# Batch 0's keys turned two tokens at a time and earlier; batch 1's values loaded ahead of W2's last quarter

## The chip, the cores and the metric

The kernel runs on one core of one Trainium2 chip. The metric is device time in microseconds, from launch to end. The engines are named as the profile names them: PE (TensorE, products), PEld (its weight loads), DVE (VectorE), ACT (ScalarE), POOL (GpSimd) and SP (SyncE, which only issues transfers here).

## The reference

Two layers follow each other. The first is attention in blocks, in which keys and values are mixed between blocks by a matrix P (five rounds of exp and of row and column scaling of `sort_net`):

```python
k_sorted = np.einsum('bhij,bhjcd->bhicd', P, k_b)      # v_sorted likewise
scores = scale * np.matmul(q_b, k_sb.transpose(0, 1, 2, 4, 3))
attn = np.exp(scores) / sum(np.exp(scores))            # in each block of 96 tokens
x = np.matmul(attn, v_sb)
```

The second is a residual MLP with affine scalings:

```python
a1 = alpha1 * x + beta1
u = x + lam * (w_tok @ a1)                             # over the 768 tokens
a2 = alpha2 * u + beta2
out = u + lam * (np.maximum(a2 @ w_ch1, 0.0) @ w_ch2)  # 512 -> 2048 -> 512
```

There are 4 batches, 8 heads, 768 tokens in 8 blocks of 96, and 64 channels a head. Inputs and output are float32.

## The kernel before, in words

**Order.** The Python program writes one stream of instructions for each engine, and a wrapper (`Engine`, L55) holds each engine to the order in which the calls stand. Its line, L65, is the one that nearly all rows of the profile carry, so rows are told apart by their tiles. Waits between engines are put in by the framework from who writes and who reads which tile. Which buffer of a pool a tile gets is also decided there.

**Accumulators.** Products go to two pools of accumulators: `psA` with 2 large ones (two banks each) and `psB` with 4 small ones (one bank each). `psa(...)` and `psb(...)` take one. A new tile waits until the readers of the tile that had its buffer are done.

**Batch 0's attention** is unlike that of the other batches, as it starts with nothing loaded. Heads go in pairs, four groups g = 0 to 3. For each group:
- `k_turn` (L387, `turn_slab` L238): keys times the mixing matrix `bigK`, which transposes them on the way. A token's keys of one head (64 rows by 64 channels) are the weights, one product a token and head: 24 products of 64x64 weights a group, into two small accumulators.
- `k_copy` (L390): two copies of 128x384 (one on DVE, one on ACT) put the turned keys into `KT0`, laid out by token.
- `score` (L414): 8 products for each half hf of the blocks, then the exp on ACT, in one instruction of 768 columns if the product went to a large accumulator, in two of 384 if it went to two small ones.
- `pv_first` (L464): attention times values, 24 products into a large accumulator, then on DVE a reciprocal and a scaling that write `x128`.

In source the turn of groups 0 and 1 stands ahead of the scores of groups 0 and 1 (L923 to L942). Then come `prep_scales` (two small DVE operations, read from the first `tok_copy` on), POOL's loads, `pv_first(0)`, and only then the turn and the copies of groups 2 and 3 (L960 to L965) and their scores. The scores of group 1 go to small accumulators, with one product on zeros (a filler, L421) ahead of them.

After that come `wtok` (transposes of `w_tok`, copied by DVE and ACT), `first_mm` (the first token products) and the rest of the MLP, which is planned by hand: `put(b, hf, "h" or "c", n, f)` hangs a piece of other work behind the n-th step of the hidden (`h`) or output (`c`) products. The next batch's attention is spread over these steps.

**Loads.** POOL issues nearly all of them, in source order: q, v and k of batch 0, `w_tok`, three scale vectors, W1 in four quarters, W2 in four quarters (L956), then for batch 1 the values, the keys (`load_kv(1)`, L987) and the queries. The values of batch 1 are first used by `mix_v(1, 0)` behind step h 13 of batch 0; the W2 quarters by `scale_weights(g)` on DVE at steps h 10, 11, 12 and 12 (L1061).

Of the kernel before, what the change touches and what calls it, by code (L numbers as in the profile page):

```python
# [7 lines left out]
FT = mybir.dt.float32  # L8
# [8 lines left out]
def kernel(  # L17
# [31 lines left out]
    HB = BLK // 2  # L49
# [23 lines left out]
    pe = Engine(nc.tensor)  # L73
    dve = Engine(nc.vector)
    act = Engine(nc.scalar)
# [11 lines left out]
    def psa(shape, dtype, name):  # L87
        return pools["psA"].tile(shape, dtype, name=name, tag="psA")

    def psb(shape, dtype, name):  # L90
        return pools["psB"].tile(shape, dtype, name=name, tag="psB")

    def const(shape, dtype, name):
        return wts.tile(shape, dtype, name=name, tag=name)

    wz = const([128, 512], F16, "wz")
# [13 lines left out]
    KT0 = att.tile([128, H4, NB, 128], F16, name="kT0", tag="tw", bufs=2)  # L110
# [3 lines left out]
    k8 = att.tile([128, H4, 12 * D], F16, name="k8", tag="raw", bufs=2)  # L114
# [77 lines left out]
                qn_of[b][:, kt, :, :], q[b, :, kt * 128:(kt + 1) * 128, :].rearrange("h p d -> p h d"),  # L192
            )

    def load_kv(b):
        for kv, src in ((1, v), (0, k)):
            raw = att.tile([128, HB, D], F16, name="raw", tag="raw", bufs=2)
            load_halves(raw, src[b])
            raw_of[(b, kv)] = raw
# [72 lines left out]
    def prep_scales():  # L272
        dve.tensor_tensor(
            ab2col[:, 3 * CT:4 * CT], ab2col[:, 2 * CT:3 * CT], ab2col[:, 3 * CT:4 * CT], ALU.mult
        )
        dve.tensor_tensor(ab2col[:, 4 * CT:5 * CT], ab2col[:, 0:CT], ab2col[:, 3 * CT:4 * CT], ALU.mult)
# [44 lines left out]
    bigK = {}  # L321
# [65 lines left out]
    def k_turn(b, g, ps):  # L387
        return turn_slab(k8, lambda r, g: bigK[b][r, g, :], g, "k_ps", ps)

    def k_copy(b, g, ps, half, eng):  # L390
        eng(
            KT0[:, g, :, :].rearrange("p i (th u) -> p (i th) u", th=2)[:, :, 0:HB].rearrange(
                "p x (c t) -> p x c t", t=12
            )[:, :, :, half * 6:half * 6 + 6],
            ps[half].rearrange("p (t x c) -> p x c t", t=6, c=4),
        )

    def v_mm(b, n, out_):
        for s in range(8):
            for th in range(2):  # L400
                d = (s + 4 * th) % 8
                r = slice(th * 64, th * 64 + 64)
                pe.matmul(
                    out_[r, d * 64:d * 64 + 64], VD[r, n * 8 + d, :],
                    bigV[b][r, :, :].rearrange("p h i -> p (h i)"), start=True, stop=True,
                )
# [54 lines left out]
        dve.tensor_tensor(dst, x_of[b][rows, kts, c], al, ALU.mult)  # L461
        dve.tensor_tensor(dst, dst, be, ALU.add)

    def pv_first(g):  # L464
        if g == 0:
            x_of[0] = moep.tile([128, 8, C], F16, name="x128", tag="x128", bufs=1)
        ps = psa([128, 2, 512], FT, "x_ps")[:, :, 0:480].rearrange("p a (k d) -> p a k d", d=80)
        for i in range(NB):
            for h2 in range(2):
                et = ets[(0, g, i // 4)][:].rearrange("p a i t -> p (a i t)")  # L470
                lo = (4 * h2 + i % 4) * BLK
                w = min(128, 8 * BLK - lo)
                val = Vs[:, (2 * g + h2) * NB + i, 0:D + 1]
                if i < 6:
                    pe.matmul(ps[0:w, h2, i, 0:D + 1], et[:, lo:lo + w], val, start=True, stop=True)
                else:
                    for a in range(3):
                        pe.matmul(
                            ps[96:128, h2, 3 * (i - 6) + a, 0:D + 1], et[:, lo + a * 32:lo + (a + 1) * 32], val,
                            start=True, stop=True,  # L480
                        )
        rc = att.tile([128, 2, 6], FT, name="rc", tag="rc", bufs=3)
        dve.reciprocal(rc[:], ps[:, :, :, D])
        dve.tensor_tensor(
            x_of[0][:, 0:NT, g * 128:(g + 1) * 128].rearrange("p k (a d) -> p k a d", a=2),
            ps[:, :, :, 0:D].rearrange("p a k d -> p k a d"),
            rc[:].rearrange("p a k -> p k a").unsqueeze(3).to_broadcast([128, NT, 2, D]), ALU.mult,
        )
# [406 lines left out]
    copy = dve.tensor_copy  # L895
# [42 lines left out]
    k_copy(0, 1, kp1, 1, act.copy)  # L938
    score(0, 0, 0, psa)
    score(0, 0, 1, psa)  # L940
    score(0, 1, 0, psb, 1)
    score(0, 1, 1, psb)  # L942
    prep_scales()
    pool.tensor_tensor(brow[0:1, :], bet1[:], lam1[:], ALU.mult)
    for j in range(1, 4):
        sp.dma_start(brow[32 * j:32 * j + 1, :], brow[0:1, :])
# [7 lines left out]
        pool.dma_start(W1p[:, :, g * 512:(g + 1) * 512], w1v[:, :, g * 512:(g + 1) * 512])  # L954
    permute(1, pool.tensor_copy, 0, 6)
    for g in range(4):  # L956
        pool.dma_start(W2p[:, g * 4:(g + 1) * 4, :], w2v[:, g * 4:(g + 1) * 4, :])
    moe_start(0)
    a1_of[0] = moep.tile([128, 8, C], F16, name="a1", tag="a1", bufs=1)
    pv_first(0)  # L960
    kp2 = k_turn(0, 2, psb)
    kp3 = k_turn(0, 3, psb)
    for g, kp in ((2, kp2), (3, kp3)):
        k_copy(0, g, kp, 0, copy)
        k_copy(0, g, kp, 1, act.copy)  # L965
    score(0, 2, 0, psa)
    score(0, 2, 1, psb)
    pv_first(1)
# [15 lines left out]
    first_turn(2, psa)  # L984
    scale_affine(betaB)

    load_kv(1)  # L987
    load_q(1)
    pool.memset(Vs[0:BLK, :, D:GRP], 1.0)

# [23 lines left out]
    for b in range(1, B):  # L1014
        p = b - 1
# [42 lines left out]
        put(b, 0, "h", 4, lambda b=b: moe_cross(b, 1))  # L1058
        put(b, 0, "c", 2, lambda b=b: moe_affine(b, 1))

    for g, m in enumerate((10, 11, 12, 12)):  # L1061
        put(0, 0, "h", m, lambda g=g: scale_weights(g))
    for n, at_ in enumerate(((0, 1, "c", 4),) * 3 + ((0, 1, "c", 5),) * 3 + ((0, 1, "c", 6),) * 2):
        put(*at_, lambda n=n: block_weights(n))
# [68 lines left out]
```

## Time and profile before

| what | us |
|---|---|
| timed runs: median (lowest to highest) of 3 | 258.17 (256.55 to 260.22) |
| the profiled execution | 256.33 |
| its span, first to last instruction | 254.6 |
| PE busy in the span | 244.0 (96%) |
| DVE, ACT, POOL busy | 174.1 (68%), 155.7 (61%), 46.1 (18%) |
| mean granted PE clock | 0.993 of full |

The profile is one execution. Its page has numbered parts: 1 is busy time, 2 cuts the span into 40 equal slices (a digit is the busy share in tenths, PEclk the granted clock in tenths), 4 is the chain of work that ended last, 5 the costliest groups. In the rows of the timeline the two numbers in front are start and duration, `xN` is the number of instructions merged into the row, and the brackets name the idle time before it and who ended it; "issue" there means that the engine waited for nothing that the profile shows.

The stretch around the change, from the timeline of before (us from the start of the span):

| work | start | length |
|---|---|---|
| scores of group 0 | 16.77 | 0.59 |
| filler, scores of group 1 | 17.29, 18.13 | 0.91, 0.51 |
| six exps of groups 0 and 1 | 17.25 | 3.05 |
| attention product of group 0 | 18.58 | 1.02 |
| turn of groups 2 and 3: one product, then 47 | 19.53, 21.22 | 0.21, 0.94 |
| their four copies, on ACT and DVE | 21.79 | 1.06 |
| scores of group 2 | 22.54 | 0.63 |
| attention product of group 1 | 23.09 | 1.64 |
| scores of group 3, transposes of `w_tok` | 24.66, 25.42 | 0.82, 1.59 |
| first token product | 26.95 | 1.14 |

### The profile page before, as it was taken

To read this page: it belongs to the slowest core of one execution; us is meant where nothing else is said; L and a number is where in the kernel's file an instruction comes from. 1 tells how busy PE (TensorE), PEld (TensorE's weight loads), DVE (VectorE), ACT (ScalarE), POOL (GpSimd) and SP (SyncE) were. 2 spreads that over 40 slices of the span, in tenths; PEclk is the share of its full clock that TensorE was granted. 3 is DMA by queue.
4 is the path that set the end of the run, shared out by engine and by line. 5 is a ranking of instruction groups with operands and counts; after the bars stand their busy time and mean duration, and the time that the engine had idled before them with its cause. 6 is when DMAs were issued, how large, how long until landed. Compare 5 with 4: busy or idle time off the path is not lost.

```text
span 254.6 us, 6059 instructions
## 1 busy us (share of the span) xinstructions
PE 244.0 (96%) x2416; PEld 159.7 (63%) x2416; DVE 174.1 (68%) x461; ACT 155.7 (61%) x285; POOL 46.1 (18%) x70
## 2 busy tenths in 40 slices
PE   7897999999999999999999999999999999999994
PEld 2475765555465545556765797558756875686783
DVE  5884588667379868279896685398978862462773
ACT  4796675567788679786564696878364005837400
POOL 8699604000082010191000010000000000000000
PEclk9997999999999999999999999999999999999999
DMA  5999999998999997999961179710203132111023
GB/s 98 202 210 192 207 205 210 216 179 197 165 179 180 131 209 124 178 159 164 136 161 39 31 189 127 141 23 0 85 0 66 50 115 45 21 41 44 0 85 82
DMA packets 61936, 31.09 MB, mean 122 GB/s; under 512 B 50562, under 2 KB 57618, under 8 KB 61908
## 3 DMA queue, kind: packets, MB, share of 16 engines
q0 software_dynamic: 20976, 16.91, 45.7%
q1 hardware_dynamic: 40836, 13.76, 32.0%
q8 instruction: 19, 0.31, 0.5%
q14 instruction: 9, 0.07, 0.1%
q10 hardware_dynamic: 96, 0.03, 0.1%
HBM read 32.79 MB, written 8.65 MB: 163 GB/s over the span
## 4 chain that ended last, share of the span: by engine, by line
PE 77%; DVE 9%; ACT 6%; DMA 3%; issue 2%; POOL 1%; DVEq 0%; ACTq 0%; POOLq 0%
PE h_ps L65 28%; PE tok_ps L65 12%; PE px L65 8%; PE ch_ps L65 8%; PE pz L65 6%; PE py L65 5%; DMA v<-in_v_dram 3%; PE x_ps L65 3%; DVE x L65 3%; PE sc_ps L65 2%; DVE sums L65 2%; PE kmix_ps L65 2%; PE mix_ps L65 2%; ACT kT L65 1%; ACT vd L65 1%
## 5 line engine op out<-in xcount | busy, mean ns | idle before, releaser
L65 PE MATMUL h_ps<-a2T,W1p 128*128 128x384 bf16 x512 | 93.4, 326 | 0.3 <-DVE a2T L65 0.3
L65 PEld LDWEIGHTS <-W1p 128*128 128x128 bf16 x512 | 47.8, 98 | 30.7
L65 ACT ACTIVATE hTa<-h_ps 128x384 f16<-128x384 f32 x64 | 31.2, 490 | 30.6 <-PE h_ps L65 29.5
L65 ACT ACTIVATE hTb<-h_ps 128x384 f16<-128x384 f32 x64 | 31.3, 489 | 8.7 <-PE h_ps L65 8.7
L65 DVE SCALAR_TENSOR_TENSOR u<-tok_ps,x 128x512 f32<-128x512 f32 x21 | 14.5, 692 | 27.0 <-PE tok_ps L65 27.0
L65 PE MATMUL tok_ps<-a,w_tokT 128*128 128x512 f16 x126 | 30.3, 379 | 0.0
L65 ACT CAST kT<-kmix_ps 64x512 f16<-64x512 f32 x36 | 25.7, 713 | 7.0 <-PE kmix_ps L65 6.5
L65 ACT ACTIVATE et<-sc_ps 96x768 f16<-96x768 f32 (+2 forms) x36 | 24.6, 736 | 2.4 <-PE sc_ps L65 2.4
L65 ACT CAST u<-u 128x512 f16<-128x512 f32 x21 | 13.0, 618 | 20.4 <-DVE u L65 20.4
L65 PEld LDWEIGHTS <-sums 128*128 128x128 f16 x216 | 21.1, 98 | 3.8 <-issue 0.7
L65 PEld LDWEIGHTS <-hTa 128*128 128x128 f16 x192 | 18.2, 98 | 6.6
L65 PEld LDWEIGHTS <-hTb 128*128 128x128 f16 x200 | 18.5, 98 | 6.1
L65 PEld LDWEIGHTS <-w_tokT 128*128 128x128 f16 x126 | 12.3, 98 | 13.1 <-DVE a L65 0.3
L65 DVE TENSOR_TENSOR x<-x_ps,rcb 96x512 f16<-96x512 f32 x24 | 16.5, 687 | 0.8
L65 DVE TENSOR_TENSOR sums<-hTa,hTb 128x512 f16<-128x512 f16 (+2 forms) x27 | 8.9, 330 | 10.3 <-ACT hTb L65 10.0
L65 PEld LDWEIGHTS <-et 96*128 96x128 f16 (+4 forms) x288 | 12.6, 103 | 2.7
L65 DVE SCALAR_TENSOR_TENSOR ost<-px,u 128x256 f32<-128x256 f32 x27 | 11.3, 419 | 3.4 <-PE px L65 3.4
L65 PE MATMUL x_ps<-Vs,et 96*128 96x65 f16 (+4 forms) x288 | 13.5, 199 | 0.0
L65 PE MATMUL ch_ps<-W2p,hTa 128*128 128x512 f16 x48 | 11.9, 380 | 0.0
L65 PE MATMUL ch_ps<-W2p,hTb 128*128 128x512 f16 x48 | 11.7, 379 | 0.0
L65 POOL DMA_DIRECT2D qn<-in_q_dram x12 | 10.7, 915 | 5.2 <-DMA raw<-in_v_dram 4.8
L65 PE MATMUL sc_ps<-qT,kT 64*128 64x96 f16 (+1 forms) x256 | 10.0, 210 | 1.5 <-DVE x L65 0.7
(140 smaller groups left out, 351.2 us busy)
## 6 DMA issues: line engine op xcount, KB each, us to landing
out_dram<-ost SPq DMA_DIRECT2D x23, 192.0 KB, 2.4
raw<-in_v_dram POOLq DMA_DIRECT2D x6, 384.0 KB, 8.4
raw<-in_k_dram POOLq DMA_DIRECT2D x6, 384.0 KB, 10.8
Vs<-vscr SPq DMA_DIRECT2D x3, 768.0 KB, 7.9
W1p<-in_moe_w_ch_dram POOLq DMA_DIRECT2D x4, 512.0 KB, 11.6
W2p<-in_moe_w_ch_dram POOLq DMA_DIRECT2D x4, 512.0 KB, 15.6
qn<-in_q_dram POOLq DMA_DIRECT2D x12, 128.0 KB, 11.1
vscr<-mixed POOLq DMA_DIRECT2D x4, 384.0 KB, 5.0
```

The source lines that it names most:

```text
L65: ins = getattr(self.eng, name)(*args, **kwargs)
```

## The change

Four things are done.

1. Groups 2 and 3 are turned by `k_turn_pairs`: the weights are the keys of two tokens at a time (64 rows by 128 columns), so there are 12 products a group in place of 24. The two tokens come out in the two halves of the partitions, and each head's accumulator is copied by `k_copy_pairs` in two copies of 64x384 that write every second token's place: four copies a group in place of two.
2. The turn of group 2 and its copies (two on DVE, two on ACT) now stand between the scores of group 0 and those of group 1, the turn of group 3 and its copies (four on DVE) behind the scores of group 1, all of it ahead of `pv_first(0)`. The scores of group 1 go to large accumulators and lose their filler; `pv_first(0)` gets one, of 480 columns, written into its own accumulator. `prep_scales` moves behind `pv_first(0)`.
3. The two loads of batch 1's values are issued ahead of W2's fourth quarter; the keys stay where they were.
4. `scale_weights(3)` is hung behind step h 15 instead of 12.

```diff
--- before.py
+++ after.py
@@ -192,8 +192,9 @@
                 qn_of[b][:, kt, :, :], q[b, :, kt * 128:(kt + 1) * 128, :].rearrange("h p d -> p h d"),
             )
 
-    def load_kv(b):
-        for kv, src in ((1, v), (0, k)):
+    def load_kv(b, *kvs):
+        for kv in kvs or (1, 0):
+            src = (k, v)[kv]
             raw = att.tile([128, HB, D], F16, name="raw", tag="raw", bufs=2)
             load_halves(raw, src[b])
             raw_of[(b, kv)] = raw
@@ -394,6 +395,27 @@
             )[:, :, :, half * 6:half * 6 + 6],
             ps[half].rearrange("p (t x c) -> p x c t", t=6, c=4),
         )
+
+    def k_turn_pairs(g):
+        ps = [psb([128, 384], FT, "k_ps")[:] for a in range(2)]
+        for tp in range(6):
+            for h2 in range(2):
+                r = slice(h2 * 64, h2 * 64 + 64)
+                pe.matmul(
+                    ps[h2][:, tp * 64:tp * 64 + 64], k8[r, g, tp * 128:(tp + 1) * 128], bigK[0][r, g, :],
+                    start=True, stop=True,
+                )
+        return ps
+
+    def k_copy_pairs(g, ps, h2, eng):
+        dst = KT0[h2 * 64:h2 * 64 + 64, g, :, :].rearrange("p i (th u) -> p (i th) u", th=2)[:, :, 0:HB].rearrange(
+            "p x (c t) -> p x c t", t=12
+        )
+        for par in range(2):
+            eng(
+                dst[:, :, :, par::2],
+                ps[h2][par * 64:par * 64 + 64, :].rearrange("p (t x c) -> p x c t", t=6, c=4),
+            )
 
     def v_mm(b, n, out_):
         for s in range(8):
@@ -461,10 +483,14 @@
         dve.tensor_tensor(dst, x_of[b][rows, kts, c], al, ALU.mult)
         dve.tensor_tensor(dst, dst, be, ALU.add)
 
-    def pv_first(g):
+    def pv_first(g, fillers=0):
         if g == 0:
             x_of[0] = moep.tile([128, 8, C], F16, name="x128", tag="x128", bufs=1)
-        ps = psa([128, 2, 512], FT, "x_ps")[:, :, 0:480].rearrange("p a (k d) -> p a k d", d=80)
+        ps = psa([128, 2, 512], FT, "x_ps")[:, :, 0:480]
+        z = wz[:].bitcast(FT)[:, 0:240]
+        for _ in range(fillers):
+            pe.matmul(ps[:, 0, :], z[:, 0:128], z.unsqueeze(1).to_broadcast([128, 2, 240]), start=True, stop=True)
+        ps = ps.rearrange("p a (k d) -> p a k d", d=80)
         for i in range(NB):
             for h2 in range(2):
                 et = ets[(0, g, i // 4)][:].rearrange("p a i t -> p (a i t)")
@@ -938,9 +964,14 @@
     k_copy(0, 1, kp1, 1, act.copy)
     score(0, 0, 0, psa)
     score(0, 0, 1, psa)
-    score(0, 1, 0, psb, 1)
-    score(0, 1, 1, psb)
-    prep_scales()
+    kp2 = k_turn_pairs(2)
+    k_copy_pairs(2, kp2, 0, copy)
+    k_copy_pairs(2, kp2, 1, act.copy)
+    score(0, 1, 0, psa)
+    score(0, 1, 1, psa)
+    kp3 = k_turn_pairs(3)
+    k_copy_pairs(3, kp3, 0, copy)
+    k_copy_pairs(3, kp3, 1, copy)
     pool.tensor_tensor(brow[0:1, :], bet1[:], lam1[:], ALU.mult)
     for j in range(1, 4):
         sp.dma_start(brow[32 * j:32 * j + 1, :], brow[0:1, :])
@@ -954,15 +985,13 @@
         pool.dma_start(W1p[:, :, g * 512:(g + 1) * 512], w1v[:, :, g * 512:(g + 1) * 512])
     permute(1, pool.tensor_copy, 0, 6)
     for g in range(4):
+        if g == 3:
+            load_kv(1, 1)
         pool.dma_start(W2p[:, g * 4:(g + 1) * 4, :], w2v[:, g * 4:(g + 1) * 4, :])
     moe_start(0)
     a1_of[0] = moep.tile([128, 8, C], F16, name="a1", tag="a1", bufs=1)
-    pv_first(0)
-    kp2 = k_turn(0, 2, psb)
-    kp3 = k_turn(0, 3, psb)
-    for g, kp in ((2, kp2), (3, kp3)):
-        k_copy(0, g, kp, 0, copy)
-        k_copy(0, g, kp, 1, act.copy)
+    pv_first(0, 1)
+    prep_scales()
     score(0, 2, 0, psa)
     score(0, 2, 1, psb)
     pv_first(1)
@@ -984,7 +1013,7 @@
     first_turn(2, psa)
     scale_affine(betaB)
 
-    load_kv(1)
+    load_kv(1, 0)
     load_q(1)
     pool.memset(Vs[0:BLK, :, D:GRP], 1.0)
 
@@ -1058,7 +1087,7 @@
         put(b, 0, "h", 4, lambda b=b: moe_cross(b, 1))
         put(b, 0, "c", 2, lambda b=b: moe_affine(b, 1))
 
-    for g, m in enumerate((10, 11, 12, 12)):
+    for g, m in enumerate((10, 11, 12, 15)):
         put(0, 0, "h", m, lambda g=g: scale_weights(g))
     for n, at_ in enumerate(((0, 1, "c", 4),) * 3 + ((0, 1, "c", 5),) * 3 + ((0, 1, "c", 6),) * 2):
         put(*at_, lambda n=n: block_weights(n))
```

## The prediction

> **What bounds the kernel now.** I read the page's parts 1, 2 and 4 first, then the chain of waits in order of time, then the timeline from 16 to 27 us, busy time in stretches of 3.41 us, and the landing times of the loads. TensorE is busy for 96% of the span and holds 77% of the chain; from 27 us on its row in the page is solid, so whatever the front of the kernel gains or loses is carried to the end. The one soft place in the part that the change edits is the fourth slice of part 2:
>
> ```profile
> PE   7897999999999999999999999999999999999994
> PEclk9997999999999999999999999999999999999999
> ```
>
> The chain (start, duration, what) shows that place close by:
>
> ```profile
> 17.35 2.96 ACT et L65 x6
> 20.31 0.91 issue
> 21.22 0.59 PE k_ps L65 x23
> 21.83 0.57 DVE kT L65
> 22.54 0.63 PE sc_ps L65 x16
> 23.16 1.57 PE x_ps L65 x24
> 24.73 0.76 PE sc_ps L65 x16
> 25.49 1.53 PE wtok_ps L65 x18
> ```
>
> Six exps, then 0.91 us in which nothing that is shown is waited for, then the key turn of groups 2 and 3, its copies, scores, and the second attention product (24 products, 1.57 us). The timeline shows what 24 such products take without trouble, and how the turn stands still:
>
> ```profile
> 18.58 1.02 PE L65 MATMUL x_ps<-Vs,et 128*128 128x65 f16 x24
> 19.52 0.10 PEld L65 LDWEIGHTS <-k 64*64 64x64 f16 x1
> 21.22 0.83 PEld L65 LDWEIGHTS <-k 64*64 64x64 f16 x47 [1.59 <-issue]
> 23.09 1.64 PE L65 MATMUL x_ps<-Vs,et 128*128 128x65 f16 x24
> ```
>
> One key weight load goes at 19.52, the other 47 only from 21.22. The windows view (stretch, length, busy us of PE, PEld, DVE, ACT, POOL, then granted clock) shows the consequence:
>
> ```profile
> 15.98:19.39 3.41, 3.33 (x88) 2.40 (x83) 2.16 (x6) 3.41 (x9) 3.01 (x6) 1.00 1.16 210
> 19.39:22.80 3.41, 1.56 (x68) 1.31 (x66) 2.16 (x4) 1.77 (x5) 3.41 (x4) 1.00 1.20 165
> 22.80:26.21 3.41, 3.41 (x60) 2.94 (x54) 1.46 (x4) 2.59 (x6) 3.41 (x5) 0.50 1.16 220
> ```
>
> A stretch in which TensorE was busy for 46% is followed by one at clock 0.50. That drop costs 1.64 - 1.02 = 0.62 us on the product and some 0.4 on the 32 scores (0.63 + 0.82 against twice 0.51): 1.0 in all. So the before kernel loses here 0.9 (the stall) and 1.0 (the clock). The question is how much of the 1.9 the new order gets.
>
> **Part 1: the stall.** The load at 21.22 has no wait of its own in the program; its exps were done by 20.31. The page's instruction row (19 packets, 0.31 MB, so 16 KB each, for 4832 TensorE instructions) and narrow windows of the DMA view, which put those packets at 11.9, 18.8, 25.2 and 31.3 us, suggest that TensorE was out of instructions and waited for a block. If so, the block boundary stays at the same count of instructions, which after the change falls behind the first of group 0's attention products, and the block is there at 21.22 as before, since nothing ahead of 17.3 us changes. If the stall belongs to the key turn, it goes. The sum below is the same in both, because the new filler covers TensorE until then. [...]
>
> **Part 2: the new chain, step by step.** TensorE does the group 2 turn at 17.3 instead of the filler (0.84 us, 17.29 to 18.13). Its keys land at 5.28 + 11.3 = 16.6, margin 0.7. It waits for the last value copy on DVE (17.45). It is 12 products on 64x128 weights instead of 24 on 64x64; the nearest row, 16 score products with such weights in 0.44 us, gives 27 ns each, 0.33 us a group. Scores of group 1 now take the two large accumulators and wait for the exps of group 0 (18.07 and 18.77): done by 19.1, and group 3's turn by 19.4.
>
> ACT is then the chain. Exps of 768 follow each other at 18.77 - 18.07 = 0.70 us. Before group 1's exps ACT must now make two key copies of 64x384 that write every second element. No row shows that shape. Lower bound: the present copies of 128x384 start 0.38 apart (21.79, 22.17). Upper: the late batches' copy writes every second key too, and costs almost twice as much per element:
>
> ```profile
> L65 ACT CAST kT<-kmix_ps 64x512 f16<-64x512 f32 x36 | 25.7, 713 | 7.0 <-PE kmix_ps L65 6.5
> ```
>
> They follow each other at 0.71; by 384/512 that is 0.54, which I take as the nearest; unscaled 0.71 is the far end. So ACT ends the copies at 18.77 + 2 x 0.54 = 19.85 and the first exp of group 1 at about 20.57 (20.25 to 20.9).
>
> The first attention product waits for just that exp, since its accumulator is the one the exp reads; before, it ran at 18.58. Its filler: the start-up ones (512 columns) step at 0.85 us (weight loads at 2.21, 3.06), so 480 columns take 0.80: 20.62 to 21.42. That is past 21.22, the stall's end, so the stall is hidden and the filler costs 0.2. Then 24 products (0.9 to the next start): scores of group 2 begin at 22.32, first half done 22.75; its exp 22.80 to 23.61 (815 ns row). In the changed program the second attention product waits for that exp, whose accumulator it takes over: 23.66, 1.02 us at full clock, done 24.68. DVE's reciprocal for it starts at 24.73. Before:
>
> ```profile
> 24.77 0.23 DVE L65 RECIPROCAL rc<-x_ps 128x12 f32<-128x12 f32 x1 [1.92 <-PE x_ps L65]
> ```
>
> So the gain is 0.04 us, between +0.25 and -0.3 by the copies' bounds. The 1.9 us are given back in three places: two more ACT copies ahead of the exps (1.08), the filler (0.8), and the exp of group 2 (0.85) that stands between two attention products and used to lie beside the first. After 24.7 both programs have the same order and waits: scale, six copies of w_tok, first token product (26.95 before).
>
> What is hidden: DVE makes six key copies where it made two; the last four start at 19.5 and at 0.47 apart (0.71 at worst) end by 21.5 (22.4), with group 3's scores at 24.7 and the next reciprocal at 22.4 behind them; without that cover 0.2 to 1.9 us. The two small scalings now come after group 0's scale, some 24.0; ACT reads them first at 28.12. SP's queue is passed by nothing that waits.
>
> **Part 3: the loads.** POOL's loads land in the order of issue, each after the one before: W2's quarters at 25.72 + 12.8 = 38.5 to 27.92 + 18.2 = 46.1, the values at 48.1 and 31.21 + 18.7 = 49.9. With the values ahead of the last quarter, they land at some 45.7 and 47.6 and the quarter at 49.9. Its issue must now wait for the same W1 landing that holds the second value load to 31.21; behind it on POOL stand only key loads that wait for TensorE until 40.76, so nobody is late. The values are first used at 50.62: margin 0.7 before, 3.0 after, and no wait is shown there, so nothing is gained. The quarter is scaled on DVE from 53.9, so 4 us are spare. Moving its scaling three steps later in the source leaves DVE's order as it was. Keys (53.6, used 56.62) and queries (55.7, used 58.23) would let a front gain of up to 2.5 us through.
>
> **Sum.** 256.33 us of the profiled execution (span 254.6, 1.7 around it) - 0.04 = 256.3. The three timed runs have their median at 258.17, 1.84 higher, so 258.1 there. No change.
>
> **The rivals.**
> *Slower: the clock drop moves instead of going.* In the stretch 19.39 to 22.80 I now count TensorE busy for 2.3 us (67%), in the next 2.3 again, as it waits for ACT at 19.4, 22.5 and between w_tok's transposes. Stretches at 83% and more kept clock 1.00, 46% lost it; what decides lies between. If the second loses it, 26.21 to 29.62 runs at 0.50, where TensorE was busy all of 3.41 us at full clock: +1.7 us, 259.8. If the first does, +1.0. For: two weak stretches instead of one. Against: both are nearer to 83 than to 46. [...]
> *Faster: the before's timed runs lose more to the clock than its profile does.* A drop that begins at 21.2 would also catch the key turn and both scores. If the new order never drops, such runs give up 1.0 to 1.5 us: 256.9. For it: the timed runs lie above the profiled one. Against: that can have any cause.
> *The change does not reach what it says.* The early values are hidden anyway, and the turn ahead only swaps one idle place for another: this is in the forecast.
> *Keys land late.* At over 17.3 instead of 16.6 the turn blocks group 1's scores, which stand behind it; a landing 1.7 us later costs 1.0.
>
> **Chances.** Forecast, within 0.6 us of no change: 0.5. Faster rival 0.26. Clock rival 0.17, late keys 0.04. Something worse than 5 us on either side 0.03. About 2% (5.2 us) is what a measurement of this kernel can tell from no change, and no priced case reaches it: faster 0.03, same 0.93, slower 0.04. The timed runs of before spread -1.6 to +2.1 around their median; with the rivals' -1.2 and +1.7 the range is 255.4 to 260.6.
>
> **What would show it.** Right: ACT with two key copies of over 0.5 us ahead of group 1's exps; TensorE idle from 19.4 to about 20.6, then the filler; the second attention product 1.0 us long and starting near 23.7; DVE's second reciprocal at 24.7. Wrong: clock 0.50 anywhere in 20 to 30 us; the second product at 23.0 or before (then the gain is 0.7 or more); a wait for the values at 50, or for W2's last quarter at 54.

## The result, and the profile after

| | before | changed |
|---|---|---|
| median of the timed runs, us (22 of each) | 257.25 | 258.75 |
| lowest to highest, us | 255.69 to 260.76 | 256.63 to 262.11 |
| ratio | | 1.0049, 95% interval 1.0026 to 1.0072 |

The ratio leaves out the slow runs, those more than 1.5% above the fastest of their kernel (four of before, eight of the changed one), so it is below that of the two medians (1.0058).

The changed kernel is slower by about 1.3 us (0.0049 x 257.25), where 0.04 us of gain and no visible change were forecast. The median lies inside the range, which says little, as the range is as wide as the scatter of the runs. The sign is not that of the forecast.

The profiled execution of the changed kernel took 261.17 us (span 259.4), longer than most of its timed runs: batch 0's values landed some 0.9 us later than in the other profile of it, and from its last VectorE operation to the end are 1.9 us more. So its total isn't compared, only its front, and a second profile of the same kernel (span 255.8, below) serves for the steps. The busy rows of the page of after, 40 equal slices, for TensorE and its granted clock:

```profile
PE   7776999999999999999999999999999999999991
PEclk9997999999999999999999999999999999999998
```

The fourth slice is still the soft one, and still has the low clock. The chain of waits of after (start, duration, what):

```profile
18.32 1.41 ACT et L65 x2
...
19.76 0.58 ACT kT L65
...
20.35 0.58 ACT kT L65
...
20.95 0.82 ACT et L65
...
21.82 2.88 PE x_ps L65 x26
...
25.18 0.82 ACT et L65
...
26.04 1.00 PE x_ps L65 x24
```

This is the foretold chain: two key copies on ScalarE (0.58 each) ahead of group 1's first exp, then filler and first attention product, and the exp of group 2 between the two attention products. The `issue` of 0.91 us is gone from it. New is that filler and product together take 2.88 us. The windows view says why (stretch, length, busy us of PE, PEld, DVE, ACT, POOL, granted clock, DMA share, GB/s):

```profile
19.00:22.41 3.41, 1.46 (x30) 1.00 (x30) 2.80 (x6) 3.35 (x6) 3.41 (x4) 1.00 1.19 180
22.41:25.82 3.41, 3.04 (x42) 2.13 (x41) 1.33 (x3) 0.70 (x2) 3.41 (x5) 0.50 1.15 206
```

TensorE was busy for 1.46 of 3.41 us (43%) while ScalarE worked without a break, and the next stretch ran at half clock. In the kernel before, the same happened after the stall. In the second profile of the changed kernel the clock stays full, and another wait can be seen. Its timeline (start, length, engine, operation, `xN` merged):

```profile
20.77 1.07 PE L65 MATMUL x_ps<-wz 128*128 128x480 f32 x2 [1.50 <-ACT et L65]
21.68 1.01 PE L65 MATMUL x_ps<-Vs,et 128*128 128x65 f16 x24
...
23.87 1.00 PE L65 MATMUL x_ps<-Vs,et 128*128 128x65 f16 x24 [0.73 <-ACT et L65]
...
23.87 1.63 DVE L65 TENSOR_TENSOR ab2col<-ab2col 128x4 f32<-128x4 f32 x2
25.42 0.22 DVE L65 RECIPROCAL rc<-x_ps 128x12 f32<-128x12 f32 x1
...
23.23 2.24 POOL L65 COPY wp<-wt 128x1728 f16<-128x1728 f16 x2
```

The second attention product ends at 24.87, but VectorE's reciprocal of it starts only at 25.42: it stands behind the two small scalings (128x4 elements each), which take 1.63 us and end when GpSimd's second permutation copy ends (23.23 + 2.24 = 25.47 by its row). That copy is two instructions, the row's x2: the first scaling (1034 ns) ends with the first of them, the second (561 ns) with the second. In the kernel before, where no copy ran beside them, the same two operations take 0.35 us:

```profile
17.83 0.35 DVE L65 TENSOR_TENSOR ab2col<-ab2col 128x4 f32<-128x4 f32 x2
```

At the first token product this profile is 0.53 us behind the one of before (27.48 against 26.95), at the last VectorE operation 1.27 (252.52 against 251.25).

### The profile page after: what moved, and what is told of

Read it like the earlier page. It is cut to its first block, busy times and chain, and to the rows that moved or that the text cites. A ratio compares the mean times of both kernels' runs of the same rounds, so it can differ in the third digit from the quotient of the medians.

```text
span 259.4 us, 6011 instructions
## 1 busy us (share of the span) xinstructions
PE 244.3 (94%) x2392; PEld 159.1 (61%) x2392; DVE 176.3 (68%) x465; ACT 156.0 (60%) x283; POOL 46.1 (18%) x70
## 4 chain that ended last, share of the span: by engine, by line
PE 78%; ACT 7%; DVE 6%; DMA 4%; SPq 2%; issue 1%; POOL 0%; DVEq 0%; POOLq 0%
PE h_ps L65 30%; PE tok_ps L65 11%; PE px L65 8%; PE pz L65 6%; PE py L65 5%; PE ch_ps L65 5%; PE x_ps L65 4%; DMA q<-in_q_dram 3%; PE sc_ps L65 2%; SPq L65 2%; ACT kT L65 2%; ACT et L65 2%; PE mix_ps L65 1%; DVE x L65 1%; DVE a2T L65 1%
## 5 line engine op out<-in xcount | busy, mean ns | idle before, releaser
L65 PEld LDWEIGHTS <-kT 64*128 64x128 f16 (+1 forms) x256 | 6.7, 97 | 7.7 <-issue 4.4
```

The costliest lines, as they stand in the source:

```text
L65: ins = getattr(self.eng, name)(*args, **kwargs)
```

## The experiments

Ratios are to the kernel before, run on the same chip, with 95% intervals. The last column counts timed runs whose mean granted clock is 0.995 or more: a stretch of 3.41 us at half clock, as long as that of before (22.80 to 26.21 us) and that of after (22.41 to 25.82), takes 3.41 x 0.5 / 255 = 0.0067 from the mean, so these are the runs with no whole such stretch (for before: all runs beside the experiments). In the 20 profiles the low stretches lie between 14 and 31 us (two pages have one more, in the last slice); where they lie in a timed run is not recorded. e7, a single run (258.98 us), is not in the table. The same program at three times (e5, e12, e14) came to 1.0144, 1.0017 and 1.0084, farther apart than the intervals of some 0.004 on either side allow. So small differences between versions measured at different times count for little.

| version | ratio | mean clock | runs without a half-clock stretch |
|---|---|---|---|
| before | | 0.996 | 74 of 132 |
| changed | 1.0049 (1.0026 to 1.0072) | 0.990 | 6 of 22 |
| changed, again (e13) | 1.0067 (1.0028 to 1.0105) | 0.990 | 3 of 12 |
| loads only (e1) | 1.0006 (0.9975 to 1.0038) | 0.995 | 6 of 12 |
| front only (e2) | 1.0109 (1.0056 to 1.0163) | 0.991 | 2 of 6 |
| no filler (e3) | 1.0122 (1.0070 to 1.0174) | 0.982 | 0 of 6 |
| group 2 copied on VectorE (e4) | 1.0059 (1.0023 to 1.0095) | 0.994 | 3 of 12 |
| scalings early (e5, e12, e14) | 1.0144, 1.0017, 1.0084 | 0.989 | 6 of 29 |
| scalings on GpSimd (e17) | 1.0104 (1.0026 to 1.0181) | 0.987 | 0 of 6 |
| fill only (e10) | 1.0054 (1.0009 to 1.0099) | 0.995 | 7 of 12 |
| scalings early, fill (e9) | 1.0028 (0.9991 to 1.0065) | 0.997 | 8 of 12 |
| scalings early, group 2 on VectorE (e8, e15) | 0.9986, 1.0008 | 0.995 | 12 of 24 |
| the same with a fill (e11) | 0.9997 (0.9958 to 1.0036) | 0.995 | 7 of 12 |
| scalings on GpSimd, group 2 on VectorE (e18) | 1.0029 (0.9988 to 1.0069) | 0.994 | 6 of 12 |
| before, scalings late (e6) | 1.0018 (0.9985 to 1.0052) | 0.990 | 0 of 12 |
| before, pairs at the old place (e16) | 1.0045 (1.0013 to 1.0078) | 0.990 | 0 of 12 |

### Loads or front

e1 is the kernel before with the change's loads alone, e2 the changed kernel with the loads put back.

```diff
 e1, on the kernel before (cut: load_kv takes the list of loads, as in the change)
+        if g == 3:
+            load_kv(1, 1)
         pool.dma_start(W2p[:, g * 4:(g + 1) * 4, :], ...)
-    load_kv(1)
+    load_kv(1, 0)
-    for g, m in enumerate((10, 11, 12, 12)):
+    for g, m in enumerate((10, 11, 12, 15)):
 e2: the same lines undone in the changed kernel
```

> The kernel before with only parts 3 and 4: batch 1's values ahead of W2's last quarter, that quarter scaled three steps later in the source. Theory (the loss sits in the front, in the chain exps, key copies, filler, two attention products): nothing waits for the values or the quarter, so within 0.4 us of before. Rival (the loads cost): the quarter lands later or its issue holds POOL up, 0.8 to 1.3 us slower than before.

> The changed kernel with the loads put back as before: parts 1 and 2 alone. Theory (front): all of the loss, 0.9 to 1.6 us slower than before, first token product some 1.4 us later against the scores of group 0 than in before. Rival (loads): about the same as before.

The loads alone cost and bring nothing that shows (1.0006); the front alone has the loss (1.0109). That is 2.8 us where 0.9 to 1.6 were expected, and more than the whole change lost; with six runs its interval (1.0056 to 1.0163) overlaps that of the whole, and the excess stays unexplained. Both profiles ran without a half-clock stretch, so they show the old and the new front at the same clock. In e1 the second attention product starts at 22.49, in e2 at 23.95; the first token product at 25.62 and 27.86. But the second token product is at 28.69 in e1, only 0.40 before the profile of before (29.09), which had lost 0.62 on the second attention product to the clock. The weight loads of e1 show what takes the rest back:

```profile
20.72 0.83 PEld L65 LDWEIGHTS <-k 64*64 64x64 f16 x47 [1.10 <-issue]
...
27.51 0.83 PEld L65 LDWEIGHTS <-et 128*128 128x128 f16 x22 [1.15 <-issue]
```

Counted in the program, the second stall stands 256 TensorE instructions behind the first, to within a product, and neither has a wait of its own. In e2 it isn't seen, as its front comes there later. So at equal clock the new front is 2.24 us late at the first token product and 29.99 - 28.69 = 1.30 at the second. Of e2's delay this much is VectorE's:

```profile
23.95 1.93 DVE L65 TENSOR_TENSOR ab2col<-ab2col 128x4 f32<-128x4 f32 x2
25.79 0.23 DVE L65 RECIPROCAL rc<-x_ps 128x12 f32<-128x12 f32 x1
...
23.41 2.25 POOL L65 COPY wp<-wt 128x1728 f16<-128x1728 f16 x2
```

The first scaling took 1732 ns, to the end of GpSimd's copy, and the second 161 ns behind it; the product had ended at 24.95, so the reciprocal is 0.84 late.

### Filler and copies

```diff
 e3
-    pv_first(0, 1)
+    pv_first(0)
 e4
-    k_copy_pairs(2, kp2, 1, act.copy)
+    k_copy_pairs(2, kp2, 1, copy)
```

> The changed kernel without the filler product ahead of the first attention product. Theory A (the filler is on the path): it ran 1.22 us at the falling clock and hid at most 0.3 us of the wait for instructions, so 0.5 to 0.9 us faster than the changed kernel. Rival B (the filler keeps the clock up or hides the wait): the same or slower, as the clock then drops over the same or a longer stretch.

> The changed kernel with the two ACT copies of group 2's keys moved to DVE, so that ACT goes from the exps of group 0 straight to those of group 1 (DVE then makes eight copies of 0.58 us, the last done some 4.7 us after the first, ahead of group 3's scores). Theory: the copies are 1.17 us of the chain; the first attention product may start 1.2 us sooner, but its instructions come at about 22 us on the scale of the changed kernel, so 0.2 to 1.2 us faster than it. If the clock drop alone makes the loss, a shorter idle time of TensorE ahead of it should also show clock 1.00 through 22 to 27 us, and the whole 1.2 us back. Rival (ACT's copies lie beside other work): no difference.

Without the filler it is no faster (1.0122), and the mean clock is the lowest of all (0.982; slices 4 and 5 of its page stand at 5 and 6 tenths). So the filler isn't the loss. With the copies on VectorE, ScalarE goes straight from group 0's exps to group 1's (four in 2.96 us, from 17.26) and the filler starts at 19.57 instead of 20.77, in that profile at half clock. 1.0059 is no gain on the changed kernel, where 0.2 to 1.2 us were expected; its scalings still ran into GpSimd's copy (566 and 744 ns).

### The scalings, moved in both kernels

```diff
 e5, e12, e14, on the changed kernel
+    prep_scales()
     kp2 = k_turn_pairs(2)
     ...
     pv_first(0, 1)
-    prep_scales()
 e6, on the kernel before
-    prep_scales()
     ...
     pv_first(0)
+    prep_scales()
     kp2 = k_turn(0, 2, psb)
```

> The changed kernel with the two small scalings (prep_scales) put back ahead of group 2's turn, all else as it is. Theory (the scalings, 128x4 from SBUF, wait on VectorE for the end of GpSimd's second permutation copy, and the reciprocal of the second attention product waits behind them): the two take 0.35 us near 18 us, the second reciprocal starts within 0.2 us of the end of its product (some 25.0 us instead of 25.8), the first token product is 0.8 to 0.9 us earlier than in the run with only the front, and the whole is 0.8 to 1.0 us shorter than the changed kernel: ratio to the kernel before 0.998 to 1.003. Rival (the loss is the longer chain or the TensorE clock, and the scalings only fill a wait that is there anyway): the reciprocal stays late and the ratio stays at 1.004 to 1.008.

> The kernel before with only the two small scalings moved, behind the first attention product and ahead of the key copies of group 2. Theory (a VectorE operation from SBUF to SBUF waits for a GpSimd copy that is running): they fall into GpSimd's first permutation copy (19.9 to 22.1 us in the kernel before), take 1.2 to 1.5 us instead of 0.35, and the first key copy on VectorE begins at 22.1 to 22.4 instead of 21.83, so 0.3 to 0.6 us are lost: ratio 1.001 to 1.003. Rival (the scalings were slow for another reason): they take 0.35 us and the key copies begin at 21.8; ratio 1.000.

e6 shows the same wait in the other program, against the other of GpSimd's copies. Its timeline:

```profile
20.87 1.35 DVE L65 TENSOR_TENSOR ab2col<-ab2col 128x4 f32<-128x4 f32 x2
22.14 1.01 DVE L65 CAST kT<-k_ps 128x384 f16<-128x384 f32 x2
...
19.76 2.24 POOL L65 COPY wp<-wt 128x1728 f16<-128x1728 f16 x2
```

The first scaling takes 1153 ns and ends with the copy at 22.0, the second takes 161 ns, and the key copies begin at 22.14 instead of 21.83. The time, 1.0018, doesn't tell the foretold 0.3 to 0.6 us from nothing. e6 also has the mean clock of the changed kernel (0.990) and no run without a low stretch, at 1.0018 (0.9985 to 1.0052): a low mean clock by itself need not cost 1.3 us. One of these 128x4 scalings took 161 ns with no copy beside it and up to 2210 ns (e14) beside one. VectorE's scaling of the product, which has one input in an accumulator, took 0.96 us beside the same copies and 0.96 without one (after, at 25.00 and 31.43).

e5's profile does what was expected of it. The scalings take 0.35 us at 17.90, the second attention product starts at 24.18 and takes 1.00:

```profile
25.21 0.23 DVE L65 RECIPROCAL rc<-x_ps 128x12 f32<-128x12 f32 x1 [0.96 <-PE x_ps L65]
```

The reciprocal follows its product at once, and the span is 254.8 us, near the 254.6 of before. Its timed runs are not near those of before: 1.0144, five of six with a clock of 0.979 to 0.993. So the expectation failed in the time, and the clock was taken up.

### Where TensorE's instructions end

```diff
 e7, on the kernel before
     warm(1)
+    tiny = psa([128, 512], FT, "warm_ps")
+    for _ in range(24):
+        pe.matmul(tiny[:, 0:64], ident16[:], ident16[:, 0:64], start=True, stop=True)
     mix_keys(0, psb)
```

> The kernel before with 24 tiny products (48 instructions of TensorE) added behind the first filler, so that every later instruction stands 48 places further on. Theory (TensorE's instructions come in blocks of 256, and the one that begins at place 687 is not there before some 21.1 us): the stall leaves the first key turn of group 2 and stands at the sixth weight load of the first attention product, which then ends near 22 us instead of 19.8; the key turn follows with no stall of its own; the first token product is some 1 us later. Rival (the key turn waits for something of its own, a load or a buffer): the stall of 1.6 us stays in front of the key turn's second weight load and the attention product ends near 20.

```profile
21.94 0.86 PEld L65 LDWEIGHTS <-et 128*128 128x128 f16 x23 [0.80 <-issue]
22.86 0.83 PEld L65 LDWEIGHTS <-k 64*64 64x64 f16 x48
```

The stall has left the key turn, whose 48 weight loads follow without a gap, and stands in the attention product 48 instructions earlier, at its second weight load (the expectation said the sixth; its places are eight too high). It belongs to the count of instructions, not to the keys. That TensorE waits for instructions is inferred; the DMA view supports it. In before, e1, e7 and e15 each such stall ends 2.3 to 2.5 us after a packet of the instruction queue starts: 18.8 and 21.22 in before, 18.45 and 20.72, then 25.15 and 27.51 in e1. This profile's values landed late too, so its times aren't compared.

### The clock, and both at once

e8 is e5 with e4's edit. e9 is e5 with two products on zeros ahead of group 3's turn, e10 the changed kernel with these alone, e11 is e8 with one. e12 is e5 again.

```diff
-    def k_turn_pairs(g):
+    def k_turn_pairs(g, fillers=0):
         ps = [psb([128, 384], FT, "k_ps")[:] for a in range(2)]
+        z = wz[:].bitcast(FT)[:, 0:192]
+        for _ in range(fillers):
+            pe.matmul(ps[0], z[:, 0:128], z.unsqueeze(1).to_broadcast([128, 2, 192]), start=True, stop=True)
...
-    kp3 = k_turn_pairs(3)
+    kp3 = k_turn_pairs(3, 2)
```

> As the run with the scalings put back early, and in addition all four copies of group 2's keys on VectorE, so that ScalarE goes straight to group 1's exponentials (theory: 1.17 us of ScalarE copies leave the chain in front of the first group 1 exponential, the filler and the first attention product start 1.2 to 1.3 us earlier, and the first token product 0.5 to 1.2 us earlier than with the scalings alone moved; ratio 0.995 to 1.000). Rival one: the next instructions of TensorE are not there before some 25 to 27 us, and the gain is given back at the second token product: ratio as with the scalings alone, 0.998 to 1.003. Rival two: the longer idle stretches of TensorE drop its clock: first attention product 1.6 us instead of 1.0, ratio 1.001 to 1.005.

> The scalings put back early, and two filler products (128x384 f32, some 0.9 us each) ahead of group 3's turn, on its own tile, where TensorE stands idle from 19.6 to 21.1 us in the run with the scalings early. Theory (the second loss is the clock, which falls after the half-idle stretch of 17.5 to 21 us): the clock stays as in the kernel before or better (mean 0.994 or more over the runs), the first attention product takes 1.0 us at an unchanged 22 us, and the time comes to that of the kernel before: ratio 0.997 to 1.002. Rival (the clock falls elsewhere or for another reason): the mean clock stays near 0.987 and the ratio at 1.004 to 1.014.

> The changed kernel, scalings late as in it, with only the two filler products ahead of group 3's turn. Theory of two losses: the clock is mended (mean 0.994 or more, where the changed kernel has 0.990), the scalings still wait for GpSimd's copy (1.3 to 1.9 us for the two) and the second reciprocal still comes 0.6 to 0.8 us behind its product: ratio 1.002 to 1.004, half to three quarters of a us below the changed kernel. If the clock is the whole loss: 0.998 to 1.001. If the scalings are the whole: 1.004 to 1.006.

> Scalings early, all of group 2's copies on VectorE, and one filler product ahead of group 3's turn. Theory: no late scalings, no half-clock stretch ahead of the first attention product, which begins near 21.2 us, bounded by the arrival of TensorE's next 256 instructions; mean clock 0.996 or more, ratio 0.994 to 0.999, the shortest of all so far. Rival (TensorE's instructions bound the front whatever is done there): ratio 0.998 to 1.002, with a stall of TensorE that the profile puts down to issue at place 687 or 943.

> The run with the scalings put back early, once more, for a second profile and more times: its profiled execution was as short as the kernel before (254.8 us, granted clock 0.999), its timed ones were 257.7 to 260.3 us in span at a clock of 0.979 to 0.993. Theory (two separate losses: the scalings, some 0.8 us, and the clock, some 1.1 us for each 0.0067 of granted clock, which is one stretch of 3.41 us at half clock): the time again goes with the clock; mean clock 0.985 to 0.992, ratio 1.003 to 1.012, and a profile with a clock below 0.99 shows the half clock between 17 and 26 us, where TensorE waits for the exponentials. Rival (the first times were chance): ratio 0.997 to 1.003 and clock 0.994 or more, as in the kernel before.

e12's profile fell at half clock, and the windows view shows the place:

```profile
17.41:20.82 3.41, 1.23 (x40) 0.94 (x39) 3.21 (x8) 3.35 (x6) 3.36 (x5) 1.00 1.17 207
20.82:24.23 3.41, 3.38 (x42) 2.49 (x43) 1.56 (x4) 0.93 (x2) 3.41 (x5) 0.62 1.15 175
24.23:27.64 3.41, 2.85 (x46) 2.54 (x47) 1.65 (x4) 2.04 (x6) 3.41 (x6) 0.50 1.22 206
```

TensorE was busy for 36% while ScalarE made exps, copies and exps without a break; then two low stretches, with 1.66 and 1.62 us for the attention products instead of 1.0. Over its timed runs e12's clock (0.991) is as its theory had it, but its ratio (1.0017) is the rival's.

The clock followed the theory: with fills, or with the scalings out of the way and the copies on VectorE, half or more of the runs have no low stretch, as in the kernel before; of the changed kernel's only 9 of 34 have none. (e4, copies on VectorE alone, lies between by its mean clock.) The time followed only in part. e10 has the clock of before and still 1.0054, near the changed kernel, where 1.002 to 1.004 was expected; e9, with the scalings early as well, 1.0028 (0.997 to 1.002 expected); e8 and e11, which also take the copies off ScalarE, 0.9986 and 0.9997, no different from the kernel before and short of the 0.994 to 0.999 hoped for in e11.

### Side by side

> The changed kernel itself, in the same call as the two versions of it that follow, so that they can be compared directly. As before: ratio 1.003 to 1.007, mean clock near 0.990, the two small scalings 0.6 to 2.0 us behind GpSimd's second permutation copy.

> The scalings early, nothing else. If they are the larger loss: 0.7 to 1.0 us below the changed kernel of the same call, ratio 0.999 to 1.003, at the same clock as it. If the clock is the larger loss, and the scalings only a smaller one or none: within 0.4 us of the changed kernel, ratio 1.003 to 1.007, at a mean clock of 0.990 or less.

> The scalings early and all of group 2's copies on VectorE. If the two losses are the scalings and the clock behind the wait for ScalarE's copies, this one has neither: mean clock 0.994 or more, ratio 0.995 to 1.001, 1.0 to 2.0 us below the changed kernel of the same call. If its first time was chance: ratio 1.002 to 1.006.

```diff
 e16, on the kernel before (cut: the two new functions, as in the change)
-    kp2 = k_turn(0, 2, psb)
-    kp3 = k_turn(0, 3, psb)
+    kp2 = k_turn_pairs(2)
+    kp3 = k_turn_pairs(3)
     for g, kp in ((2, kp2), (3, kp3)):
-        k_copy(0, g, kp, 0, copy)
-        k_copy(0, g, kp, 1, act.copy)
+        k_copy_pairs(g, kp, 0, copy)
+        k_copy_pairs(g, kp, 1, act.copy)
```

> The kernel before with the keys of groups 2 and 3 turned two tokens at a time, at their old place behind the first attention product (24 products fewer, eight copies of 0.58 us instead of four of 0.55 and 0.48). The stall for TensorE's instructions at place 687 stays at the second weight load of group 2's turn (1.6 us, to some 21.2). TensorE saves some 0.45 us of turning, ScalarE needs 1.17 us for a group's copies where it needed 0.48, so the scores of group 2 start at 22.3 to 22.7 where they started at 22.0 to 22.5: 0 to 0.5 us lost, ratio 1.000 to 1.003, the small scalings at 0.35 us. If the form alone costs what the changed kernel lost: ratio 1.004 to 1.007.

Measured side by side, the medians in us are: changed 258.95, scalings early 259.90, scalings early with the copies on VectorE 257.53, before 257.00. Over all runs, early scalings alone bring nothing that can be measured. Among runs without a half-clock stretch they do: the mean span is 255.2 us in six of them (e5, e12, e14) and 256.1 in nine of the changed kernel, a difference of 0.9 with a standard error of 0.34. With one low stretch both stand at 257.1, with two at 258.4 and 257.9. e14's timeline shows one reason why early scalings need not help, which e5's profile hid:

```profile
19.75 2.41 DVE L65 TENSOR_TENSOR ab2col<-ab2col 128x4 f32<-128x4 f32 x2
...
19.70 2.24 POOL L65 COPY wp<-wt 128x1728 f16<-128x1728 f16 x2
```

In this execution the values had landed late, all was shifted by some 1.8 us, and the early scalings met GpSimd's first copy: 2.21 us for one of them, with all six key copies of VectorE behind, from 22.08 on. With the scalings early, taking the copies off ScalarE brought the ratio from 1.0084 to 1.0008 here, and from 1.0144 to 0.9986 between e5 and e8: 2.0 and 4.1 us. With the scalings late it brought nothing (e4 has 1.0059, the changed kernel 1.0049 and 1.0067), so it is no loss that stands by itself. e16 says that the form alone, at the old place, costs about as much as the whole change (1.0045, where 1.000 to 1.003 was expected): ScalarE's four copies take 2.35 us, group 2's exp waits for them till 23.73, and no run was without a half-clock stretch.

```diff
 e17, on the changed kernel; e18 also has e4's edit
     def prep_scales():
-        dve.tensor_tensor(...)            # both
+        pool.tensor_tensor(...)
...
+    prep_scales()
     permute(0, pool.tensor_copy, 0, 6)
...
     pv_first(0, 1)
-    prep_scales()
```

> The changed kernel with the two small scalings on GpSimd itself, ahead of its first permutation copy, so that VectorE can meet that copy neither early nor late. Theory (the loss by the scalings is VectorE's wait for GpSimd's copies, here gone at every landing of the loads; the clock is left as it is): the second reciprocal starts within 0.2 us of its product's end, in runs with equal granted clock 0.5 to 0.9 us below the changed kernel, mean clock 0.988 to 0.992, ratio 1.002 to 1.005. Rival (the scalings cost nothing that stays): ratio 1.004 to 1.008.

> The same with all of group 2's copies on VectorE. Theory (both losses mended): mean clock 0.994 or more, ratio 0.995 to 1.000, the first attention product near 21 us and bounded by TensorE's instructions; of what is gained in front, up to 1.4 us is given back near 101 us, where the hidden layer of batch 1 waits for the transposing transfers of u. Rival: that wait takes all: ratio 1.000 to 1.003.

On GpSimd the scalings take 0.21 us each and meet nobody. e17 is 1.0104 all the same, with no run at full clock; e18, with the copies on VectorE, 1.0029. e17's expected ratio failed, and e18's is its rival's; by the ratios 1.9 us separate the two, which differ in ScalarE's copies alone. No version is clearly faster than the kernel before. One reason is seen in e15, whose front is 0.83 us ahead of before from the first token product (26.12) on, with a stall of TensorE's instructions at the place foretold for the changed kernel:

```profile
20.82 0.87 PEld L65 LDWEIGHTS <-et 128*128 128x128 f16 x23 [0.68 <-issue]
...
100.63 1.25 DVE L65 TENSOR_SCALAR a2T<-uT,ab2col 128x384 bf16<-128x384 f16 x4 [2.15 <-DMA uT<-u]
```

and of before:

```profile
99.96 1.25 DVE L65 TENSOR_SCALAR a2T<-uT,ab2col 128x384 bf16<-128x384 f16 x4 [0.66 <-DMA uT<-u]
```

At 101 us the hidden products wait for VectorE, and VectorE for the transposing transfer of u, which ended later than in before although all ahead of it was earlier. TensorE idles 0.93 there, and the lead of 0.83 is a lag of 0.64 at 103.5 us. In e15 one of the three transposing transfers took 2.53 us to issue (1.64 at most in before) and up to 3.8 us to land (2.4 in before); why wasn't tried. TensorE idles at this place for 0.45 us or more in eight of the 20 profiles, those of e1, e15 and both of the changed kernel among them, and not in those of before, e2 or e18.

## Why the forecast was wrong, point by point

Two steps failed: the two small scalings, put at nothing, and the 1.0 us of clock, put down as regained. The chain between them was right.

- **The stall** (part 1): right. It belongs to the count of instructions (e7), falls behind the first attention product of the changed kernel, and is covered by the filler (e15 shows it as soon as the product comes early).
- **The chain to the second attention product** (part 2): right in mechanism and nearly in size. Group 2's turn at 17.07 to 17.43 (17.3 forecast), the key copies 0.58 each (0.54, bounds 0.38 to 0.71), the second product at 23.87 and 23.95 (23.66). Two of its side sums are off, and the start times use neither: the three costs named, 1.08, 0.8 and 0.85, add up to 2.7 and not to the 1.9 given back, and 713 ns for 512 elements is 1.4 times 0.38 us for 384 per element, not almost twice.
- **"The two small scalings now come after group 0's scale, some 24.0"**, among what is hidden, costed at nothing: wrong. What was asked was who reads them, not who stands behind them on VectorE and what GpSimd does meanwhile. They wait for GpSimd's copy and hold the second reciprocal (forecast at 24.7) to 25.42 in one profile and 25.79 in another, 0.5 to 0.8 us; in the profile that landed late by 0.9 us they cost nothing, because the copy was nearly over. The wait is shown (e2, e6, e14). Its share of the measured time is shown only in part: moving the scalings alone shortened the runs at full clock by 0.9 us, and not the runs as a whole.
- **"1.0 in all" for the clock, put down as lost before and regained after**: wrong, and with the scalings it is where the sign comes from as far as the runs show. The one profiled execution of before had a low stretch, but 74 of its 132 timed runs had none; and with the same front and a full clock (e1) the kernel is just 0.40 us ahead at the second token product, as TensorE stands still again 256 instructions on. The changed kernel was taken to run at full clock; 25 of 34 of its runs have one low stretch or more. In its 34 runs the mean span is 256.1 us with none, 257.1 with one, 257.9 with two and 258.8 with three. Before: 255.4, 255.8 and 257.7 (none, one, two). So the runs at full clock differ by 0.7 us, and the rest goes with the clock; by e6 that need not make the clock its cause. Two low stretches or more (a mean clock under 0.9885) come in 16 of 34 runs of the changed kernel, in 9 of 132 of before, and in 4 of 48 with group 2's copies on VectorE (e4, e8, e15, e18). The rival "the clock drop moves instead of going" had 0.17 and a price of 1.0 to 1.7; it is the nearest to what came.
- **"In the stretch 19.39 to 22.80 I now count TensorE busy for 2.3 us (67%)"**, the ground for giving the clock rival only 0.17: the count was nearly right (2.03 us in the second profile of the changed kernel), the conclusion was not. First, the stretch was taken where the windows of before lay, and those of another execution lie elsewhere. The weakest 3.41 us of the new front are 17.4 to 20.8, under ScalarE's exps and copies. In the second profile of the changed kernel:

```profile
17.40:20.81 3.41, 1.24 (x40) 0.95 (x39) 3.02 (x6) 3.35 (x6) 3.23 (x4) 1.00 1.17 207
19.39:22.80 3.41, 2.03 (x34) 1.41 (x36) 2.29 (x5) 2.01 (x3) 3.41 (x5) 1.00 1.16 163
```

  36% there, below the 46% of before. Second, "nearer to 83 than to 46" doesn't tell what the clock does. e4 lost it with no stretch near 46%:

```profile
16.00:19.41 3.41, 2.63 (x89) 1.94 (x81) 3.37 (x7) 3.41 (x8) 3.40 (x6) 1.00 1.16 210
19.41:22.82 3.41, 3.25 (x26) 2.05 (x26) 3.08 (x6) 0.81 (x2) 3.41 (x5) 0.53 1.19 167
```

  The drop is at 19.6, and the 3.41 us ahead of it have TensorE busy for 2.47, 72%. In e8 and e18 it is 71%. The profile above, at 36%, kept the clock, and so did e5's at 33%. With the copies off ScalarE the weakest stretch is no longer that low (e15: 2.32 us, 68%) and the runs with two low stretches become rare, but one low stretch still comes in half of them. What decides in a single execution isn't shown.
- **The loads** (part 3): right, nothing (e1). The values are read at 53.0 us in the profile of after with no wait for them; W2's last quarter is waited for by nobody.
- **"Whatever the front gains or loses is carried to the end"**: only nearly. In the second profile of the changed kernel the lag of 0.53 at the first token product is 0.52 at 98 us, 1.5 at 103 after the wait for the transposing transfer, and 1.27 at the end.
- **The range**: its lower end adds the spread of the runs and the rival's gain to the forecast (258.2 - 1.6 - 1.2 = 255.4). Its upper end, added up alike, would be 262.0, not 260.6. The median lies inside either.

What stays open: how the 1.3 us divide between scalings and clock. At full clock the changed kernel is 0.7 us longer in span than before, and 0.9 longer than with the scalings early. That points to the scalings for all of the 0.7, but on six and nine runs, picked out afterwards. Also open is why the same program differs so much from one time of measurement to another. One part of the scatter may be the landing of batch 0's loads: the scores of group 0 start between 16.70 and 19.32 us in the 20 profiles, and no timed run says when they did.

## What to carry to other kernels

When a small operation is moved, look at both sides of its queue, and at what the other engine does at its new place: two 128x4 multiplications are 0.35 us or 2.4 us, by whether GpSimd copies at that moment. A clock that falls in the one profiled execution is a chance per run (58 of the 132 timed runs of before), not a term of the sum: read from the timed runs' clocks how often it falls, and ask of a change whether it makes the half-idle stretches ahead of it longer. Where one engine's work is put in front of another's (here ScalarE's copies in front of the exps that TensorE waits for), count the idle time of the waiting engine too.

## What the runs showed of the hardware that was not expected

- TensorE's weight loads stood still with nothing shown to wait for at places 256 instructions apart: 1.10 and 1.15 us at two of them in e1, 1.59 us at the first in before. The DMA row of before's page stands at 9 tenths around it (slices 2 to 8).
- The granted clock fell to half after stretches of 3.41 us with TensorE busy for 36 to 46% (e12, after, before), and also after 71 and 72% (e8, e18, e4). It stayed full after 33 to 36% (e5, e2, e13). In e3 it stayed low for more than one stretch (0.67, 0.50 and 0.50 in three). TensorE's longest idle time between two products ahead of the drop was 1.48 us in before and 1.51 in after; the clock stayed full after one of 1.51 in e5 and of 1.50 in e13.
- A ScalarE copy of 64x384 that writes every second element takes 0.58 us. One of 128x384, as many elements a partition on twice the partitions, written in runs of six, takes 0.48.
